# Batch 1's fifth group of attention weights turned by TensorE in place of a transposing DMA, and the eighth group's turn one step earlier

## The chip, the cores and the metric

The kernel runs on one core of one Trainium2 chip. The metric is the device time of one execution in microseconds, the median of several runs. The kernel before takes 306.03 us (three runs, 305.89 to 306.10).

A core has five engines with an instruction stream each: TensorE (PE: matmuls, with the weight load PEld beside it), VectorE (DVE), ScalarE (ACT), GpSimd (POOL) and SyncE (SP). Each works through its stream in order and waits on semaphores for the others. Here SP and POOL issue nearly all DMAs.

## The reference

Sliding-window causal attention, and behind it a two-layer network whose activation is h * cos(h):

```
scores = scale * np.matmul(q, k.transpose(0, 1, 3, 2))      # q, k, v: (8, 8, 576, 64)
rel = pos[:, None] - pos[None, :]
mask = (rel >= 0) & (rel < 64)
scores = np.where(mask, scores, -1e9)
attn = exp(scores - max) / (sum + 1e-09)
x = (attn @ v).transpose(0, 2, 1, 3).reshape(4608, 512)
h = x @ w_in                                                # (4608, 2048)
out = (h * np.cos(h)) @ w_out                               # (4608, 512)
```

## The kernel before, in words

**Two interleaved jobs.** The 4608 rows of x are cut into nine macro tiles of 512 rows. A macro tile `mt` runs the network: 16 column blocks of 128 of `h` (function `first`, four accumulating matmuls into a PSUM bank, L351), then `sin(h + pi/2)` on ACT (L527) and `h * sin` on DVE (L530), giving `gT`; then the second product, 64 matmuls `out_ps` (L542) into the two banks O0 and O1, copied out and stored. Attention for the batches ahead is put between these matmuls, so that PE always has something to do.

**Groups and units.** Eight batches, four head pairs `p` each, nine 64-row blocks `j` per batch. A unit is (batch, pair, block): two heads side by side, a 128x128 tile of scores. Groups hold three or four units. In the stage that this change touches (macro tile 0, getting ready macro tile 1) there are twelve groups, counted here from one, while the code's `i` counts from zero: the first (last block of batch 0) and the second (block 6 of batch 1) have four units, the third to the tenth have three (blocks 0 to 2 and 3 to 5 of one pair each), the eleventh and twelfth have four (blocks 7 and 8). In order of pairs: third = pair 0 blocks 0 to 2, fourth = pair 1 blocks 0 to 2, fifth = pair 0 blocks 3 to 5, sixth = pair 1 blocks 3 to 5, seventh and eighth = pairs 2 and 3 blocks 0 to 2, ninth and tenth = pairs 2 and 3 blocks 3 to 5.

**Steps of a group.** Scores on PE (`burst`, L261); on DVE, mask and maximum (`g_max`, L277); on ACT, exponential and sum (`g_exp`, L288); on DVE, the reciprocal of the sums (`g_inv`, L295); on POOL, the normalised bf16 weights `w` (`g_norm`, L302; on DVE for the first two groups). Then `w` has to be turned, since the product with the values needs it transposed (`wT`). `g_trans` has two ways: a group whose index is in `direct` is turned by PE, one 128x128 transpose per unit against the identity into a PSUM tile `tw_ps` (L311), and `g_put` copies that on DVE to SBUF as `wT` (L109); all others are turned by one DMA that SP issues (L314). `values(mt, p)` multiplies `wT` with the values for one pair (16 small matmuls, L330), and `put_x` copies the result to `xT` (on ACT for pair 1, on DVE for the others, L109), which is the operand of the `h` matmuls.

**Where the order comes from.** Nothing reorders instructions: `at(time, fn, ...)` puts a step on a list with a planned time, and `pump(time)` emits all steps up to a time between two column blocks or four `out_ps` matmuls. Steps emitted earlier stand earlier on every engine that they use. `LAGS` gives the distance of a group's steps from its scores, `DIRECT` names the groups that PE turns, `late` shifts the turn of some by one step, and `ready` says from when a unit's `wT` may be used, from which the time of `values` follows.

**Buffers.** PSUM has three rotating tiles with the tag `t` (`tw_ps`, `o_ps`), and the named banks X0, X1, S, O0, O1. The first five `h` blocks of macro tile 1 go into X0, X1, S, O0 and O1 in this order (`H_SECOND`), the last two of which hold macro tile 0's `out_ps` until DVE (O0) and ACT (O1) have copied them out.

**Loads.** POOL issues the DMAs that bring q, k (`rows`, L149) and v (L162) of later batches, in its one queue with the `w` of L302. SP issues the turns of `w`, the turns of a whole batch's q and k rows (`T`, L153), copies within v (L170) and the stores (L384).

Of the kernel before, what the change touches and what calls it, by code (L numbers as in the profile page):

```python
# [33 lines left out]
T = 2 * Q  # L34
LAGS = (0.2, 1, 3, 3.2, 3.8)
SKEW = 3
DIRECT = (0, 1, 5, 7, 8, 9)

# [11 lines left out]
def kernel(  # L52
# [18 lines left out]
    n_mt = B * S // MT  # L71
# [150 lines left out]
    groups = [[(0, p, j) for j in range(GF * g, GF * g + GF)] for p in range(PAIRS) for g in range(TU // GF)]  # L222
# [3 lines left out]
    for b, cuts in enumerate(CUTS, 1):  # L226
        for cut in cuts:
            for p0 in range(0, PAIRS, 2):
                for of, lo, hi in cut:
                    groups += [[(b, p, j) for p in range(p, p + of) for j in range(lo, hi)] for p in range(p0, p0 + 2, of)]  # L230
    direct = set(range(n_first)) | {n_first + i for i in DIRECT}

# [155 lines left out]
    def at(time, fn, *args):  # L388
        plan.append((time, len(plan), fn, args))
# [8 lines left out]
    ready = {(0, p, j): 0 for p in range(PAIRS) for j in range(TU)}  # L398
    n = n_first
    for t in range(B - 1):  # L400
        last = max(i for i, units in enumerate(groups) if units[0][0] == t + 1)
        time = T * t + Q - 1.4
        times = [time]
        for i in range(n, last + 1):
            times.append(times[-1] + PACE * len(groups[i]))
        if t:
            at(times[0], burst, n, BURSTS[0])
            at(times[4] + 0.1, burst, n + 4, BURSTS[1])
        else:
            for i in range(0, last + 1 - n, 2):  # L410
                at(times[max(i - 1, 0)] + (0.5 if i else 0), burst, n + i, (S_BANKS[i % 3], S_BANKS[(i + 1) % 3]))
        for i in range(last + 1 - n):
            time = times[i] + (0.3 if i > 3 and t else 0)
            lags = LAGS[:2] + tuple(T * t + T - 0.79 - time + 0.01 * s for s in range(3)) if n == last and t else LAGS
            if not t and i in (2, 3):
                lags = LAGS[:2] + (2.3, 2.5, LAGS[4])
            if not t and i == 9:
                lags = LAGS[:2] + (2.62, 2.63)
            for lag, fn in zip(lags, (g_max, g_exp, g_inv)):
                at(time + lag, fn, n)  # L420
            if t or i > 1:
                at(time + lags[3], g_norm, n)
            else:
                at(time + lags[2] + 0.01, g_norm, n, "d")
            late = 1 if not t and i in (5, 7) else 0
            at(time + (4.6 + late if n in direct else lags[-1]) if not t or i < 6 else T * t + T + 0.1 * i, g_trans, n)
            if n in direct:
                at(time + (4.62 if not t and i > 7 else 4.9) + late, g_put, n)
            ready.update({unit: time + (5.9 if n in direct else 8.5 if t else 9.6) for unit in groups[n]})
            n += 1  # L430

    for i, (name, p0) in enumerate((("q", 0), ("k", 0), ("q", 2), ("k", 2))):
# [16 lines left out]
    for mt in range(1, n_mt):  # L449
        for p in range(PAIRS):  # L450
            time = max(ready[b, p - p % 2 + i // TU, j] for i in range(2 * TU) for b, j in (divmod(mt * TU + i % TU, NU),))
            time = max(time, 25.5) if mt == 1 else T * mt - (8.01 if mt == n_mt - 1 else 1.01)
            at(time, values, mt, p)
            if mt == 1:
                at(time + 0.3 + 0.2 * (p % 2), put_x, mt, p, "a" if p == 1 else None)
            else:
                at(time + 0.2 + 0.1 * p, put_x, mt, p, "a" if p == 1 else None)
# [127 lines left out]
```

## Time and profile before

| what | value |
| --- | --- |
| median of three runs | 306.03 us (305.89 to 306.10) |
| the profiled execution | 306.36 us, of it 304.3 us span |
| PE busy | 292.8 us, 96% of the span |
| ACT busy | 235.6 us, 77% |
| DVE busy | 218.5 us, 72% |
| POOL busy | 170.9 us, 56% |
| granted TensorE clock | 0.999 |
| turns of `w` by DMA | 66, of them six in the stage of macro tile 1 |

The span is the time from the first to the last instruction of the profiled execution; some 2 us of the device time lie outside it. PE is busy for nearly all of the span, so the span can shrink by what PE waits, or by what it need not do. The page's chain of waits goes back from the last instruction to what released each step. A row of the timeline gives the start, the time taken, the engine, the line, the operation, the number of merged instructions, and in brackets the idle time before it with its releaser. Matmuls overlap in the pipeline, so the distance from one start to the next tells more of what an instruction costs than its own duration.

### The profile page before, as it was taken

What the parts mean: (1) busy time and instruction counts of PE and PEld (TensorE: products, weight loads), DVE (VectorE), ACT (ScalarE), POOL (GpSimd) and SP (SyncE); (2) the same over time, 40 slices, a digit from 0 to 9 for tenths busy, and PEclk for the clock granted to TensorE, in tenths of its full rate; (3) what the DMA queues carried; (4) which work ended last, traced back from release to release, by engine and by line L of the source; (5) the groups of instructions that cost most, each with busy time, mean ns of one, the idle gap of its engine ahead of it and who ended that gap; (6) DMA issues with size and microseconds to landing.
All of it is one profiled execution on the core that took longest, in us unless ns stands there. A gap on an engine that the chain in (4) does not pass through costs nothing.

```text
span 304.3 us, 7982 instructions
## 1 busy us (share of the span) xinstructions
PE 292.8 (96%) x2696; PEld 146.8 (48%) x2736; DVE 218.5 (72%) x834; ACT 235.6 (77%) x786; POOL 170.9 (56%) x198
## 2 busy tenths in 40 slices
PE   7899999899999999999999999999999999999996
PEld 6665444444454444444544444444444454454443
DVE  3877888678787878787877787778788877236701
ACT  5998799877997799679987998799869986106600
POOL 8996249794667867695649864977443630000000
PEclk9999999999999999999999999999999999999999
DMA  7999999999969996999999999999994433011011
GB/s 150 176 211 207 207 154 175 146 143 221 149 136 148 212 171 125 155 188 206 123 153 172 207 135 170 152 216 132 166 142 156 85 81 112 0 72 70 2 69 69
DMA packets 165577, 43.88 MB, mean 144 GB/s; under 512 B 154720, under 2 KB 160800, under 8 KB 165536
## 3 DMA queue, kind: packets, MB, share of 16 engines
q0 software_dynamic: 99344, 18.06, 76.1%
q1 hardware_dynamic: 66048, 25.11, 42.6%
q8 instruction: 21, 0.34, 0.5%
q10 hardware_dynamic: 144, 0.20, 0.2%
q14 instruction: 20, 0.16, 0.2%
HBM read 36.70 MB, written 9.44 MB: 152 GB/s over the span
## 4 chain that ended last, share of the span: by engine, by line
PE 73%; POOL 10%; DMA 9%; issue 4%; DVE 2%; ACT 1%; POOLq 0%; DVEq 0%
PE h_ps L351 37%; PE out_ps L542 30%; DMA w_out<-in_moe_w_out_dram 6%; POOL w L302 4%; DMA wT<-w 3%; PE o_ps L330 3%; PE s_ps L261 2%; POOL rows L142 2%; POOL rows L149 1%; POOL v L162 1%; PE out_ps L376 1%; POOL w_in L175 1%; POOL v L109 1%; DVE s L277 1%; ACT e L288 1%
## 5 line engine op out<-in xcount | busy, mean ns | idle before, releaser
L351 PE MATMUL h_ps<-xT,w_in 128*128 128x512 bf16 x557 | 125.9, 379 | 1.5 <-issue 0.3
L542 PE MATMUL out_ps<-w_out,gT 128*128 128x512 bf16 x542 | 123.0, 379 | 1.9 <-issue 1.1
L530 DVE TENSOR_TENSOR gT<-h_ps,sin 128x512 bf16<-128x512 f32 x144 | 95.4, 689 | 34.0 <-ACT sin L527 33.7
L527 ACT ACTIVATE sin<-h_ps 128x512 f32<-128x512 f32 x144 | 82.9, 599 | 34.2 <-PE h_ps L351 32.9
L288 ACT ACTIVATE e<-s,negm 128x128 f32<-128x128 f32 x256 | 98.6, 388 | 0.3 <-DVE negm L277 0.3
L302 POOL TENSOR_TENSOR w<-e,rden 128x512 bf16<-128x512 f32 (+1 forms) x76 | 74.7, 998 | 31.8 <-DVE rden L295 30.6
L351 PEld LDWEIGHTS <-w_in 128*128 128x128 bf16 x576 | 55.7, 98 | 65.7 <-issue 1.1
L542 PEld LDWEIGHTS <-gT 128*128 128x128 bf16 x560 | 53.2, 98 | 62.4 <-issue 0.2
L277 DVE CUSTOM_DVE_ANT_0 s<-s_ps,mask 128x128 f32<-128x128 f32 x256 | 58.0, 284 | 0.0
L288 ACT ACTIVATION_READ_ACCUMULATOR e<-s,negm 128x1 f32 x256 | 48.3, 189 | 0.0
L149 POOL DMA_DIRECT2D rows<-in_q_dram x30 | 25.5, 870 | 23.3 <-DMA T<-rows 13.9
L162 POOL DMA_DIRECT2D v<-in_v_dram x35 | 29.7, 877 | 10.5 <-DMA rows<-in_k_dram 7.5
L109 ACT COPY out_sb<-out_ps 128x512 f32<-128x512 f32 (+1 forms) x18 | 10.1, 564 | 24.7 <-PE out_ps L542 19.2
L295 DVE RECIPROCAL rden<-den 128x4 f32<-128x4 f32 (+1 forms) x80 | 13.8, 172 | 19.6 <-ACT e L288 18.2
L149 POOL DMA_DIRECT2D rows<-in_k_dram x30 | 25.5, 892 | 4.0 <-DMA rows<-in_q_dram 3.2
L109 DVE CAST xT<-o_ps 128x512 bf16<-128x512 f32 x27 | 17.5, 681 | 7.3 <-PE o_ps L330 7.0
L277 DVE DVE_READ_ACCUMULATOR2_ANT negm<- 128x1 f32 x256 | 21.2, 83 | 0.0
L109 DVE COPY out_sb<-out_ps 128x512 f32<-128x512 f32 x18 | 12.4, 689 | 12.0 <-PE out_ps L542 12.0
L288 ACT ACTIVATE e<-s_ps,negm 128x128 f32<-128x128 f32 x32 | 11.5, 425 | 1.9 <-DVE negm L273 1.4
L330 PE MATMUL o_ps<-wT,v 128*64 128x64 bf16 x504 | 11.4, 197 | 1.5 <-DMA wT<-w 1.4
L261 PEld LDWEIGHTS <-T 64*64 64x64 bf16 x512 | 8.2, 106 | 8.6 <-DVE negm L277 3.9
L330 PEld LDWEIGHTS <-v 128*64 128x64 bf16 x504 | 9.6, 112 | 5.8 <-issue 3.7
(58 smaller groups left out, 155.4 us busy)
## 6 DMA issues: line engine op xcount, KB each, us to landing
out_dram<-out_sb SPq DMA_DIRECT2D x16, 512.0 KB, 6.7
v<-in_v_dram POOLq DMA_DIRECT2D x28, 128.0 KB, 8.4
rows<-in_q_dram POOLq DMA_DIRECT2D x24, 128.0 KB, 5.9
rows<-in_k_dram POOLq DMA_DIRECT2D x24, 128.0 KB, 8.5
w_out<-in_moe_w_out_dram POOLq DMA_DIRECT2D x2, 1024.0 KB, 16.2
w_in<-in_moe_w_in_dram POOLq DMA_DIRECT2D x2, 768.0 KB, 12.5
wT<-w SPq DMA_TRANSPOSE x66, 4.5
out_dram<-out_sb SPq DMA_DIRECT2D x3, 256.0 KB, 2.0
```

Of the source, the lines that this page charges most:

```text
L109: {"a": nc.scalar.copy, "p": nc.gpsimd.tensor_copy}.get(engine, nc.vector.tensor_copy)(out, in_)
L149: nc.gpsimd.dma_start(out=rows(b)[lo:lo + n, slot * 512:slot * 512 + 512].rearrange("p (h d) -> p h d", h=H), in_={"q": q, "k": k}[name][b ...
L162: nc.gpsimd.dma_start(out=vt.rearrange("p (h d) -> p h d", h=H), in_=v[b, :, c * 128:c * 128 + n, :].rearrange("h p d -> p h d"))
L261: nc.tensor.matmul(out=s_ps[cross][to, u].rearrange("p (a t) -> p a t", a=2), lhsT=q_cols(b, p, j)[d], rhs=k_cols(b, p, j)[d], start=True, ...
L277: nc.vector.tensor_tensor_reduce(out=s[:, u], in0=s_ps[:, u], in1=mask[:, 2 - j % 2 if j else 0], scale=-scale if b else -1.0, scalar=BIG, ...
L288: nc.scalar.activation(e[:, u], s[:, u], AF.Exp, bias=negm[:, u:u + 1], scale=1.0 if n < n_first else -1.0, accum_out=den[:, u:u + 1])
L302: (nc.gpsimd if engine == "p" else nc.vector).tensor_tensor(out=w[:, 0:u], in0=e[:, 0:u], op=ALU.mult, in1=rden[:, 0:u].unsqueeze(2).to_br ...
L330: nc.tensor.matmul(out=o_ps[64 * h:64 * h + 64, 64 * i:64 * i + 64], lhsT=values_of(b)[:, max(j - 1, 0), 128 * p + 64 * h:128 * p + 64 * h ...
L351: nc.tensor.matmul(out=st["h", ff], lhsT=w_in_sb[:, ks, ff * 128:ff * 128 + 128], rhs=st["xT", mt][:, ks], start=start, stop=stop)
L527: nc.scalar.activation(sin, h_ps, AF.Sin, bias=math.pi / 2.0)
L530: nc.vector.tensor_tensor(out=gt[:, e], in0=h_ps, in1=sin, op=ALU.mult)
L542: nc.tensor.matmul(out=o_ps[e], lhsT=gT[ff // 2][:, ff % 2, ms * 128:ms * 128 + 128], rhs=w_out_sb[:, ff], start=ff == 0, stop=ff == n_ff - 1)
```

## The change

```
-DIRECT = (0, 1, 5, 7, 8, 9)
+DIRECT = (0, 1, 4, 5, 7, 8, 9)
...
-            late = 1 if not t and i in (5, 7) else 0
+            late = 1 if not t and i in (4, 5) else 0
             at(time + (4.6 + late if n in direct else lags[-1]) if not t or i < 6 else T * t + T + 0.1 * i, g_trans, n)
             if n in direct:
                 at(time + (4.62 if not t and i > 7 else 4.9) + late, g_put, n)
-            ready.update({unit: time + (5.9 if n in direct else 8.5 if t else 9.6) for unit in groups[n]})
+            ready.update({unit: time + (5.9 + late if n in direct else 8.5 if t else 9.6) for unit in groups[n]})
...
-            time = max(time, 25.5) if mt == 1 else T * mt - (8.01 if mt == n_mt - 1 else 1.01)
+            time = max(time, 29.5) if mt == 1 else T * mt - (8.01 if mt == n_mt - 1 else 1.01)
```

The fifth group (index 4) joins the groups that PE turns, and its turn comes one step late. The eighth (index 7) loses its late step. The planned time of pairs 0 and 1's `values` was set by the fifth group's DMA (19.78 + 9.6 = 29.38) and is now held at 29.5; its place among PE's instructions stays. Each turn by PE brings a copy on DVE with it.

On PE, in the second half of macro tile 0, around the scores of the last two groups (`s_ps`). The rows `w_...` with L311 are turns; the fifth group's `w` is w_1180. Rows of before; there the sixth group's `w` is w_1221, the eighth's w_1277 and the ninth's w_1302:

```order
L542 MATMUL out_ps_1189<-w_out_78,gT_702 128x512
L261 LDWEIGHTS T_790 [waits DVE_49]
L261 MATMUL s_ps_1253<-T_790 64x128 [waits PE_49]
...
L542 MATMUL out_ps_1189<-w_out_78,gT_729 128x512
L311 LDWEIGHTS w_1221 [waits Pool_49]
L311 MATMUL tw_ps_1284<-ident_79,w_1221 128x128
...
L542 MATMUL out_ps_1188<-w_out_78,gT_961 128x512
L311 LDWEIGHTS w_1277 [waits Pool_49]
...
L311 LDWEIGHTS w_1302 [waits Pool_49]
```

The same place in the changed kernel; the sixth group's `w` is now w_1219, the eighth's w_1281, the ninth's w_1306:

```order
L542 MATMUL out_ps_1189<-w_out_78,gT_702 128x512
L311 LDWEIGHTS w_1180 [waits Pool_49]
L311 MATMUL tw_ps_1244<-ident_79,w_1180 128x128
...
L261 LDWEIGHTS T_790 [waits DVE_49]
L261 MATMUL s_ps_1257<-T_790 64x128 [waits PE_49]
...
L311 LDWEIGHTS w_1219 [waits Pool_49]
...
L542 MATMUL out_ps_1188<-w_out_78,gT_846 128x512
L311 LDWEIGHTS w_1281 [waits Pool_49]
...
L311 LDWEIGHTS w_1306 [waits Pool_49]
```

Three turns of the fifth group stand ahead of the last scores, and the eighth group's turns stand four `out_ps` matmuls before the ninth's instead of directly ahead of them.

On PE a little later, inside pair 0's `values`, at the first use of the fifth group's `wT` (wT_1199 before). Rows of before:

```order
L330 LDWEIGHTS v1_75 [waits DMAHW3_49,DMAHW2_49]
L330 MATMUL o_ps_1350<-wT_1144,v1_75 64x64
L330 LDWEIGHTS v1_75 [waits DMASW3_49]
L330 MATMUL o_ps_1350<-wT_1199,v1_75 64x64 [waits DMAHW6_49]
L330 LDWEIGHTS v1_75
```

And of the change, where the fifth group's `wT` is wT_1253:

```order
L330 LDWEIGHTS v1_75 [waits DMAHW3_49,DMAHW2_49]
L330 MATMUL o_ps_1356<-wT_1144,v1_75 64x64
L330 LDWEIGHTS v1_75 [waits DMASW3_49]
L330 MATMUL o_ps_1356<-wT_1253,v1_75 64x64
L330 LDWEIGHTS v1_75
```

The wait on the DMA semaphore (DMAHW6) at this matmul is gone; nothing else in front of it has moved.

On DVE, between the tenth group's maxima and the eighth group's reciprocal (one piece of the difference):

```order
 L277 ISA s,negm<-s_ps,mask 128x128
 L277 ISA negm 128x1
+L109 COPY wT<-tw_ps 128x384
 L295 RECIPROCAL rden<-den 128x3
 L277 ISA s,negm<-s_ps,mask 128x128
```

The fifth group's copy out of PSUM is new there; the eighth group's copy moves from behind the twelfth group's maxima to a place ahead of them.

## The prediction

> **What bounds the kernel now.** I read the page's busy table and the chain of waits, then PE's waits by stretch, then the timeline of PE, POOL, SP, ACT and DVE between 49 and 61 us, where the change acts.
>
> ```profile
> PE 292.8 (96%) x2696; PEld 146.8 (48%) x2736; DVE 218.5 (72%) x834; ACT 235.6 (77%) x786; POOL 170.9 (56%) x198
> PE o_ps L330 <- DMA wT<-w: 0.7, 1, 0.7
> PE out_ps L542 <- issue: 1.1, 7, 0.2
> ```
>
> The second row is what the waits of PE give for 20 to 64 us, and the same row comes once more for 92 to 123 us; the third is PE's only other entry from 60 us to the end. So PE is the bound, and behind 20 us it loses noticeable time to another engine or to a DMA in two places alone, each of them a `values` matmul that waits for a turned `w`. The chain of waits runs over the first:
>
> ```profile
> 51.15 5.49 DMA wT<-w
> 56.64 0.04 issue
> 56.68 0.57 PE o_ps L330 x24
> ```
>
> PE's timeline around it (start, us, what):
>
> ```profile
> 49.42 1.90 PE L542 MATMUL out_ps<-w_out,gT 128*128 128x512 bf16 x8
> 51.25 0.42 PE L261 MATMUL s_ps<-T 64*64 64x128 bf16 x16
> 51.60 1.04 PE L542 MATMUL out_ps<-w_out,gT 128*128 128x512 bf16 x4
> 52.47 0.33 PE L311 MATMUL tw_ps<-ident,w 128*128 128x128 bf16 x3
> 52.64 1.89 PE L542 MATMUL out_ps<-w_out,gT 128*128 128x512 bf16 x7
> 54.36 0.51 PE L311 MATMUL tw_ps<-ident,w 128*128 128x128 bf16 x6
> 54.71 1.03 PE L542 MATMUL out_ps<-w_out,gT 128*128 128x512 bf16 x4
> 55.66 0.32 PE L330 MATMUL o_ps<-wT,v 128*64 128x64 bf16 x8
> 56.68 0.57 PE L330 MATMUL o_ps<-wT,v 128*64 128x64 bf16 x24 [0.70 <-DMA wT<-w]
> 57.18 0.34 PE L311 MATMUL tw_ps<-ident,w 128*128 128x128 bf16 x3
> 58.22 1.24 PE L351 MATMUL h_ps<-xT,w_in 128*128 128x512 bf16 x5
> 59.40 0.69 PE L330 MATMUL o_ps<-wT,v 128*64 128x64 bf16 x32
> 60.02 1.25 PE L351 MATMUL h_ps<-xT,w_in 128*128 128x512 bf16 x5
> ```
>
> Eight matmuls of pair 0 run (block 8 of batch 0, blocks 0 to 2 of batch 1: the first and third groups), and the ninth, on the fifth group, waits. 32 of these matmuls with no wait take 0.62 us (59.40 to 60.02), 0.0194 each. With no wait pairs 0 and 1 would have gone from 55.66 to 56.28; the next instruction starts at 57.18. The place costs 0.90 us, not the 0.70 in the brackets, because starts that overlap in the pipeline hide some 0.2.
>
> **What the change removes.** The fifth group's DMA and the wait on it. What is late next is the fourth group's DMA: pair 1 needs it from its third matmul on, the 19th of the 32. SP's rows for the fourth and the fifth, and the landing of the third and fourth (two DMAs: lowest, median, highest; the third's alone is 4.8):
>
> ```profile
> 49.86 1.25 SPq L314 DMA_TRANSPOSE wT<-w  x1
> 51.15 1.25 SPq L314 DMA_TRANSPOSE wT<-w  x1
> DMA to landing us min/median/max: 4.8/5.6/6.4
> ```
>
> The fourth lands at 49.86 + 6.4 = 56.26. SP issues it before the fifth's, which is the one taken out, so I keep 56.26; with the 0.04 of the chain PE can go on at 56.30.
>
> **What it adds on PE.** Three turns. Turns in a row cost 0.17 for three (52.47 to 52.64) and 0.35 for six (54.36 to 54.71). Parting the eighth group's from the ninth's adds none. So +0.17.
>
> *A rule against it.* The Trainium skill (TensorE: Matmul & The Clock Gate, Part 4: PE-mode transpose) measured about 275 ns for one such transpose inside a kernel. By it three would be an estimated 0.83 us, and little of the gain would be left. The rows above disagree: at 0.058 us from start to start they run pipelined, and the measurement decides; a rival below prices turns that do not overlap.
>
> **Do the turns wait for POOL?** POOL's `w` of the fifth, eighth and ninth groups:
>
> ```profile
> 50.13 0.84 POOL L302 TENSOR_TENSOR w<-e,rden 128x384 bf16<-128x384 f32 x1
> 52.49 0.82 POOL L302 TENSOR_TENSOR w<-e,rden 128x384 bf16<-128x384 f32 x1
> 53.65 0.83 POOL L302 TENSOR_TENSOR w<-e,rden 128x384 bf16<-128x384 f32 x1 [0.34 <-DVE rden L295]
> ```
>
> The fifth's is done at 50.97, and PE comes to it at 51.25: 0.28 to spare. Then, 0.17 later each: scores at 51.42, four `out_ps` from 51.77, the sixth group's turns at 52.64, four more, the eighth's at 52.81 + 0.87 = 53.68 (its `w` is done at 53.31, 0.37 to spare), four more, the ninth's at 53.85 + 0.87 = 54.72 (`w` at 54.48, 0.24 to spare). The eighth is the one that moves ahead, by 0.68 against 54.36. Where a slack is used up, each further tenth is a tenth of PE, with the last scores queued behind; I cost it at zero.
>
> **What it adds on DVE.** One copy of 0.35, ahead of the eighth group's reciprocal, for which POOL's `w` at 52.49 waits.
>
> ```profile
> 51.79 0.08 DVE L277 DVE_READ_ACCUMULATOR2_ANT negm<- 128x1 f32 x1
> 52.10 0.18 DVE L295 RECIPROCAL rden<-den 128x3 f32<-128x3 f32 x1 [0.23 <-ACT e L288]
> 53.06 0.35 DVE L109 COPY wT<-tw_ps 128x384 bf16<-128x384 bf16 x1
> 54.41 0.18 DVE L295 RECIPROCAL rden<-den 128x3 f32<-128x3 f32 x1 [0.90 <-ACT e L288]
> ```
>
> DVE is free from 51.87 and waits for ACT until 52.10. The turns run from 51.25 to 51.42 and are through the pipeline at about 51.64 (a turn takes 0.22), so the copy runs from 51.87 to 52.22 and the reciprocal comes 0.12 later, at 52.40 done: before the 52.49 at which POOL is free. The next maxima move by 0.12, the sixth's copy and the ninth's reciprocal with them, unless the overlap of DVE's instructions swallows it; the ninth's `w` would then end at 54.60, still ahead of 54.72. The 0.90 idle before 54.41 takes up the rest and the eighth's copy is taken in behind it. If that cover were gone, 0.1 to 0.35 would be PE's at the ninth's turns.
>
> **The sum on PE.** Pair 0 starts at 55.66 + 0.17 = 55.83; the 19th matmul would come at 55.83 + 18 x 0.0194 = 56.18, waits 0.12 for the fourth group, and the last 14 take 0.27: the tenth group's turns start at 56.57 instead of 57.18, 0.61 earlier.
>
> **What gives some of it back.** ACT does not move with PE here:
>
> ```profile
> 56.97 0.39 ACT L288 ACTIVATE e<-s,negm 128x128 f32<-128x128 f32 x1
> 57.35 0.57 ACT L109 CAST xT<-o_ps 128x512 bf16<-128x512 f32 x1
> 58.42 0.58 ACT L109 COPY out_sb<-out_ps 128x512 f32<-128x512 f32 x1 [0.51 <-PE out_ps L542]
> ```
>
> Its exponentials fill it up to 57.35 whatever PE does, pair 1's cast ends at 57.92, and only then can it copy O1, which the fifth `h` matmul needs. Before, the copy ended at 59.00 and that matmul started at 58.22 + 4 x 0.216 = 59.08 (0.216: twelve `out_ps` from 51.60 to 54.36, less 0.17 of turns). Now the copy goes from 57.92 to 58.50 and the matmul comes at 58.58, not at 59.08 - 0.61 = 58.47. So 0.50 is left, at most 0.55 if the copy starts a little before the cast's end, as the cast did after its exponential. The 0.51 of idle time on ACT was the cover; it is just used up. Pair 0's cast on DVE comes earlier with PE.
>
> Behind 60 us PE has work without a break until 121, so 0.50 passes through. Span 304.3 - 0.50 = 303.8; the profiled execution 306.36 would be 305.86; it stands 0.33 above the median, so against the median I forecast 306.03 - 0.50 = **305.53**. The bounds: 0.72 if the fourth lands early and ACT's copy does not bind (0.90 less 0.17), 0.35 if 0.15 is lost at the ninth's turns.
>
> **Rivals.**
>
> The second place where PE waits for a turned `w`, in macro tile 3:
>
> ```profile
> 108.57 0.69 POOL L162 DMA_DIRECT2D v<-in_v_dram  x1 [2.41 <-DMA rows<-in_k_dram]
> 109.27 3.04 POOL L302 TENSOR_TENSOR w<-e,rden 128x512 bf16<-128x512 f32 x3
> 121.05 0.47 PE L330 MATMUL o_ps<-wT,v 128*64 128x64 bf16 x18 [0.66 <-DMA wT<-w]
> ```
>
> POOL stands behind a load whose queue slot waits for a k load, so its `w` of that batch start late. (a) *Eaten later*: if those loads do not come 0.50 earlier, PE's wait grows from 0.66 to 1.16, and the time is 306.0. Against it: the loads go back to `T`, which SP turns behind the `w` of the batch before, all fed by PE's scores. (b) *That wait shrinks*: the loads from 59.74 us on are issued earlier, since POOL's last `w` of this stage follows DVE and PE; if the k load lands relatively sooner, up to 0.66 more is gained: 304.9. Nothing in the rows but the size of POOL's 2.41 wait speaks for it.
>
> (c) *Slower*: the fourth group's DMA becomes the long wait. The landing of the six DMA turns between 30 and 70 us:
>
> ```profile
> DMA to landing us min/median/max: 4.3/5.9/7.9
> ```
>
> At 7.9 the fourth would land at 57.76; PE goes on at 57.80, the last 14 end at 58.07, 0.89 after 57.18: 306.92. The point from which it decides is 7.0 us (49.86 + 7.0 + 0.04 + 0.27 = 57.17). For it: 6.4 is already the longest of those issued by 53 us. Against: everything ahead of it in the queues stays.
>
> (d) *The turns don't overlap*, 0.22 each: +0.66 in place of 0.17, pair 0 starts at 56.32, the tenth's turns at 56.94: 0.24 gained, 305.79.
>
> **How the numbers follow.** Forecast 48%, its own range 305.3 to 305.7; (a) 11%, (b) 18%, (c) 19%, (d) 4%. 0.2%, about what a measurement can tell from no change here, is 0.61 us: faster means below 305.42, slower above 306.64. A third of the forecast's chance lies below 305.42 (the bound of 0.72, and part of (b) with it): 16%, with (b) 34% faster. (c) 19% slower. The rest, 32 + 11 + 4 = 47%, same. The range that leaves out 2 in 10 takes in (b) and (a) and the first half of (c): 304.7 to 306.4.
>
> **What would show it.** Right: the `o_ps` row near 56 us has no wait or one of about 0.1, on the fourth group's DMA; the tenth's turns start at 56.5 to 56.7; ACT's copy of O1 follows the cast without idle time; the `h` matmuls after pairs 2 and 3 start at 59.5 instead of 60.02; the wait near 120.5 us is 0.66 again. Wrong: an idle time on POOL's `w` ahead of L311, a wait over 0.5 at the 19th `values` matmul, or more than 1 us at 120.5.

## The result, and the profile after

| | before | with the change | ratio, 95% interval |
| --- | --- | --- | --- |
| first comparison | 306.10 us (16 runs) | 304.91 us (16 runs) | 0.9970 [0.9957, 0.9983] |
| repeated later (`f1_after`) | 305.75 us (35 runs) | 304.99 us (12 runs) | 0.9972 [0.9959, 0.9985] |
| repeated once more (`g3_after`) | 305.78 us (23 runs) | 305.11 us (12 runs) | 0.9984 [0.9969, 0.9998] |

The change makes the kernel faster, by 0.3% in the first two comparisons and 0.16% in the third: 1.19, 0.76 and 0.67 us, where 0.50 was forecast. Single executions of the kernel before lie between 304.5 and 306.9 us but for three outliers, those with the change between 304.4 and 306.8, so one run of each would not have told; the ratios here and below leave out the highest of those outliers, 605.71 us, and one execution of `e3_after_v`, 380.29 us at a granted clock of 0.756.

The busy table of the change's page, PE's longest wait from 20 to 64 us (second row) and its only one from 92 to 123 us (third row):

```profile
PE 291.8 (96%) x2699; PEld 145.6 (48%) x2739; DVE 219.0 (72%) x835; ACT 235.5 (78%) x786; POOL 170.3 (56%) x198
PE tw_ps L311 <- POOL w L302: 0.3, 1, 0.3
PE out_ps L542 <- issue: 0.2, 1, 0.2
```

PE's wait for a turned `w` is in neither place any more; a wait of 0.3 us for POOL is new. PE's timeline of the change around the first place (start, us, what), to be held against the one in the prediction:

```profile
51.36 0.34 PE L311 MATMUL tw_ps<-ident,w 128*128 128x128 bf16 x3 [0.33 <-POOL w L302]
52.86 0.33 PE L311 MATMUL tw_ps<-ident,w 128*128 128x128 bf16 x3
53.03 1.03 PE L542 MATMUL out_ps<-w_out,gT 128*128 128x512 bf16 x3
53.89 0.33 PE L311 MATMUL tw_ps<-ident,w 128*128 128x128 bf16 x3
56.05 0.72 PE L330 MATMUL o_ps<-wT,v 128*64 128x64 bf16 x32
56.69 0.34 PE L311 MATMUL tw_ps<-ident,w 128*128 128x128 bf16 x3
57.73 1.24 PE L351 MATMUL h_ps<-xT,w_in 128*128 128x512 bf16 x5
59.53 1.69 PE L351 MATMUL h_ps<-xT,w_in 128*128 128x512 bf16 x7
```

Pairs 0 and 1 now run as one block of 32 from 56.05, and the `h` matmuls behind pairs 2 and 3 start at 59.53 instead of 60.02: 0.49 us. The second place, in macro tile 3, on PE:

```profile
118.78 1.41 PE L330 MATMUL o_ps<-wT,v 128*64 128x64 bf16 x64
120.22 4.04 PE L351 MATMUL h_ps<-xT,w_in 128*128 128x512 bf16 x17
```

Before, these 64 matmuls were cut at 121.05 by a wait of 0.66 and the `h` matmuls began at 121.45 (121.05 and the 0.40 of the last 18). From the `h` matmuls of macro tile 1 to the start of these 64 both kernels take the same (60.02 to 119.26 before, 59.53 to 118.78 now: 59.24 and 59.25), so the 1.23 us at 120.22 are 0.49 from the first place and 0.74 from the second. Behind it nothing changes: the span went from 304.3 to 303.1. POOL ahead of the second place:

```profile
106.31 0.69 POOL L162 DMA_DIRECT2D v<-in_v_dram  x1 [0.66 <-DMA rows<-in_k_dram]
107.38 1.03 POOL L302 TENSOR_TENSOR w<-e,rden 128x512 bf16<-128x512 f32 x1 [0.38 <-DVE rden L295]
```

The last v load waits 0.66 instead of 2.41 for what the prediction calls its queue slot, and POOL's first `w` starts at 107.38 instead of 109.27: 1.89 earlier, where PE is 0.49 earlier. In the trace that slot is a DMA semaphore. POOL's loads count on eight semaphores in turn, and this load has to wait until the second k load, which counts on the same one, has landed. That k load was issued at 98.17 and had landed at 108.04 before; with the change it was issued at 98.58 and had landed at 105.78.

SP carries the delay on to PE. Its six turns of `w` in that stage, before and with the change:

```profile
110.35 8.57 SPq L314 DMA_TRANSPOSE wT<-w  x6
```

```profile
108.44 9.42 SPq L314 DMA_TRANSPOSE wT<-w  x6
```

Before, the first one starts when POOL's first `w` is done (109.27 and 1.04), and all six follow close behind one another. POOL has caught up with DVE by 112.48, SP has not: its last turn starts at 117.72, although the `w` for it was done at 117.07, and lands at 121.01, just before PE goes on at 121.05. With the change the last turn starts at 116.65, when its `w` is done (116.58).

### The profile page after: what moved, and what is told of

Read it like the earlier page. It is cut to its first block, busy times and chain, and to the rows that moved or that the text cites. A ratio compares the mean times of both kernels' runs of the same rounds, so it can differ in the third digit from the quotient of the medians.

```text
span 303.1 us, 7987 instructions
## 1 busy us (share of the span) xinstructions
PE 291.8 (96%) x2699; PEld 145.6 (48%) x2739; DVE 219.0 (72%) x835; ACT 235.5 (78%) x786; POOL 170.3 (56%) x198
## 4 chain that ended last, share of the span: by engine, by line
PE 86%; DVE 4%; POOL 4%; issue 2%; DMA 2%; ACT 1%; POOLq 0%; DVEq 0%
PE h_ps L351 41%; PE out_ps L542 36%; PE o_ps L330 3%; PE s_ps L261 3%; DMA v<-in_v_dram 2%; DVE s L277 1%; PE out_ps L376 1%; POOL rows L142 1%; POOL v L162 1%; PE tw_ps L311 1%; POOL w L302 1%; POOL v L109 1%; ACT e L288 1%; DVE w L302 0%; DVE out_sb L109 0%
## 5 line engine op out<-in xcount | busy, mean ns | idle before, releaser
L109 ACT COPY out_sb<-out_ps 128x512 f32<-128x512 f32 (+1 forms) x18 | 10.1, 563 | 24.5 <-PE out_ps L542 19.0
L261 PE MATMUL s_ps<-T 64*64 64x128 bf16 x512 | 12.1, 221 | 0.0
```

The costliest lines, as they stand in the source:

```text
L109: {"a": nc.scalar.copy, "p": nc.gpsimd.tensor_copy}.get(engine, nc.vector.tensor_copy)(out, in_)
L261: nc.tensor.matmul(out=s_ps[cross][to, u].rearrange("p (a t) -> p a t", a=2), lhsT=q_cols(b, p, j)[d], rhs=k_cols(b, p, j)[d], start=True, ...
```

## The experiments

### Is the eighth group's move part of the gain? (`e1_late8`)

```
-            late = 1 if not t and i in (4, 5) else 0
+            late = 1 if not t and i in (4, 5, 7) else 0
```

> The change with the eighth group's turn left where it was before (directly ahead of the ninth's). My theory: that move is worth nothing, since six turns in a row cost 0.35 us and twice three cost 2 x 0.17, and the eighth group's weights are not awaited by anybody until pairs 2 and 3. Time as with the change, 304.9 us (within 0.3). Rival: parting the turns is part of the gain (a turn waits for POOL's weights when the six stand together, or the order of the copies on DVE matters): 0.3 to 0.6 us above the change, and a wait of PE's turns on POOL in the trace.

Measured: 304.79 us (12 runs), beside a kernel before of 305.35 (35 runs): 0.9983 [0.9965, 1.0002], an interval that takes in 1. Its timeline on PE:

```profile
54.45 0.50 PE L311 MATMUL tw_ps<-ident,w 128*128 128x128 bf16 x6
55.74 0.69 PE L330 MATMUL o_ps<-wT,v 128*64 128x64 bf16 x32
57.41 1.34 PE L351 MATMUL h_ps<-xT,w_in 128*128 128x512 bf16 x5
59.31 2.55 PE L351 MATMUL h_ps<-xT,w_in 128*128 128x512 bf16 x10
```

Six turns stand together, none waits, and 59.31 is no later than the change's 59.53. The eighth group's move brings nothing that these runs can see.

### Is the second wait POOL's queue? (`e2_before_v`, `e3_after_v`)

The kernel before, and the change, with batch 3's last v load put behind the `w` of its stage:

```
-            at(t0 + (0.5 if b == 2 else 14) + 0.8 * c, load_v, b, c)
+            at(t0 + (33 if (b, c) == (3, 4) else (0.5 if b == 2 else 14) + 0.8 * c), load_v, b, c)
```

> The kernel before, with one load moved: batch 3's fifth v load goes behind the weights of that stage in POOL's queue. My theory: the second wait (0.66 us at 121 us) comes from POOL standing behind this load, whose queue slot waits for a k load. The wait goes, the first (0.7 us near 56.7 us) stays: 306.1 - 0.66 = 305.4 us. Rival: the weights of that stage are late for another reason (the DMA that turns them, or the k load itself): the wait stays, 306.1 us.

> The change, with the same load moved. My theory: the second wait is already gone in most executions of the change, so the move adds little to the median: 304.6 to 304.9 us, with less spread; against the kernel before with the load moved, the first wait alone is left as the difference, 0.5 us. Rival: the change's gain is one effect and the load's move another, which add up: 304.9 - 0.66 = 304.2 us.

Measured: `e2_before_v` 305.51 us, 1.0009 [0.9979, 1.0038] against the same 35 runs of before; `e3_after_v` 304.88 us, 0.9989 [0.9973, 1.0005]. PE in the profile of `e2_before_v`:

```profile
55.15 0.32 PE L330 MATMUL o_ps<-wT,v 128*64 128x64 bf16 x8
56.76 0.57 PE L330 MATMUL o_ps<-wT,v 128*64 128x64 bf16 x24 [1.29 <-DMA wT<-w]
60.10 1.69 PE L351 MATMUL h_ps<-xT,w_in 128*128 128x512 bf16 x7
119.34 1.41 PE L330 MATMUL o_ps<-wT,v 128*64 128x64 bf16 x64
```

POOL's first `w` there follows DVE instead of a load:

```profile
107.94 1.03 POOL L302 TENSOR_TENSOR w<-e,rden 128x512 bf16<-128x512 f32 x1 [2.08 <-DVE rden L295]
```

SP's last turn of the stage starts at 117.18 instead of 117.72, although PE is no earlier than before (60.10). The second wait is gone and the first is still there, as my theory has it, and its 305.57 for the profiled execution fits. But the median is not under that of the kernel before beside it. That session's kernel before was already lower than in the first one (305.35 against 306.10), which was not profiled there, so this pair says where the wait comes from and leaves open what the move is worth. On the change the move gains nothing; the two effects don't add up as the rival had it (304.2). In the profile of `e3_after_v` the fourth group's DMA holds PE, as my rival (c) had it, though for less: the `h` matmuls start 0.18 us later than before (60.20 and 60.02), where (c) had 0.89.

```profile
51.41 0.34 PE L311 MATMUL tw_ps<-ident,w 128*128 128x128 bf16 x3 [0.22 <-POOL w L302]
57.02 0.41 PE L330 MATMUL o_ps<-wT,v 128*64 128x64 bf16 x14 [0.45 <-DMA wT<-w]
60.20 1.47 PE L351 MATMUL h_ps<-xT,w_in 128*128 128x512 bf16 x6
```

### Does the second wait come back when PE is late? (`e4_pad`, `f4_pad_v`)

Nine matmuls of the identity behind the tenth group's turns, with unused results:

```
-    nc.vector.memset(small, 0.0)
+    nc.vector.memset(small, 0.0); at(29.94, warm, "X1", 9)
```

> The change, with nine matmuls of the identity (results unused) behind the tenth group's turns, some 0.5 us of PE, so that PE reaches the h matmuls of macro tile 1 when it did before. Theory A: the second wait went because everything behind 57 us comes 0.5 us earlier against the loads; now it comes back, 306.0 us. Theory B: it went because the fifth group's DMA is no longer in SP's queue, which moves the later DMAs whatever PE does; it stays away, 304.9 + 0.5 = 305.4 us.

Measured: 305.96 us (12 runs, none under 305.64), 1.0024 [1.0009, 1.0039]. PE and POOL in its profile:

```profile
60.07 1.69 PE L351 MATMUL h_ps<-xT,w_in 128*128 128x512 bf16 x7
121.12 0.47 PE L330 MATMUL o_ps<-wT,v 128*64 128x64 bf16 x18 [0.69 <-DMA wT<-w]
```

```profile
95.52 4.25 POOL L149 DMA_DIRECT2D rows<-in_q_dram  x5 [4.54 <-DMA T<-rows]
108.30 1.66 POOL L162 DMA_DIRECT2D v<-in_v_dram  x2 [1.70 <-DMA rows<-in_k_dram]
109.97 5.14 POOL L302 TENSOR_TENSOR w<-e,rden 128x512 bf16<-128x512 f32 x5
```

With PE back at 60.07 the second wait is back, 0.69, and the time is theory A's. The route is not that of before: POOL's loads begin 2.2 us later than before (95.52 against 93.30), and two v loads stand ahead of the `w`. They are also 1.3 us later against PE than with the change (95.52 - 60.07 against 93.70 - 59.53), because SP's turns of batch 3's rows, whose landing POOL waits for, take longer than in either kernel (4.67 before, 6.09 with the change):

```profile
87.81 6.69 SPq L153 DMA_TRANSPOSE T<-rows  x2
```

So the premise of theory B, that the later DMAs run otherwise without the fifth group's DMA, holds here too, and this run does not show that 0.5 us of PE alone brings the wait back. The same kernel with both of these loads behind the `w`:

```
-            at(t0 + (0.5 if b == 2 else 14) + 0.8 * c, load_v, b, c)
+            at(t0 + (30 + c if b == 3 and c > 2 else (0.5 if b == 2 else 14) + 0.8 * c), load_v, b, c)
```

> The change with the nine matmuls of padding, which brought the second wait back (0.69 us in the profile, 305.96 us), and batch 3's fourth and fifth v loads behind the weights of that stage in POOL's queue. My theory: the wait comes from POOL standing behind these loads, so it goes although PE is as late as before: 305.4 us, the change plus the padding. Rival: the weights are late for another reason: the wait stays, 306.0 us.

In this kernel the copies within v (on DVE for this batch) read batch 3's fourth piece before it is loaded, so a part of that batch's values is not the reference's; the instructions are the same in number. Measured: 305.08 us, 0.9980 [0.9967, 0.9994] beside a kernel before of 305.75, where `e4_pad` stood at 1.0024. PE and POOL:

```profile
59.32 2.55 PE L351 MATMUL h_ps<-xT,w_in 128*128 128x512 bf16 x11
118.56 1.64 PE L330 MATMUL o_ps<-wT,v 128*64 128x64 bf16 x64
```

```profile
107.16 1.03 POOL L302 TENSOR_TENSOR w<-e,rden 128x512 bf16<-128x512 f32 x1 [0.53 <-DVE rden L295]
```

The wait is gone, POOL's `w` follow DVE again. PE is earlier in this execution, too (59.32, in spite of the padding), so the single profile does not part the two causes. The medians do better, since the slowest of its 12 runs (305.65) is under the kernel before beside it (305.75) and the fastest of `e4_pad` (305.64) above its own (305.35). They differ by 0.88 us, more than the wait of 0.69, so they do not measure the wait alone. Together with `e2_before_v`, where PE is as late as before, they show that the second wait arises in POOL's queue.

### How much is the first place worth? (`f1_after`, `g1_before`, `g2_before`, `g3_after`)

Both kernels unchanged, run and profiled again.

> The change itself once more, beside the kernel before on this chip, since the kernel before came out at 305.35 us where three of its variants ran (35 runs, 304.5 to over 306), against 306.10 earlier. My theory: the kernel before sits at one of two levels, with and without the second wait (0.7 us), and the change stays at the lower one: the change 304.9 us, 0.4 to 1.2 us under the kernel before by how often that shows the wait. Rival: the 1.2 us measured first is the size of the effect and the kernel before is again at 306.1.

> The kernel before, one more profile. My theory: the fifth group's DMA pins PE near 56.7 us however early PE arrives, so the h matmuls behind pairs 2 and 3 start at 60.0 to 60.1 us again, with a wait of 0.7 to 1.3 us for that DMA. Rival: that start varies from execution to execution as it does with the change (58.96 to 60.20 us over seven profiles).

> The same once more; the second wait (near 121 us) may be there or not, and where it is not, the time is about 305.4 us instead of 306.1.

> The change, beside the kernel with the third k load moved, on the same chip: 304.9 us.

The times of `f1_after` and `g3_after` are in the first table; the single executions of the kernel before took 306.11 and 306.42 us. PE in the two profiles of the kernel before, first `g1_before`:

```profile
56.60 0.57 PE L330 MATMUL o_ps<-wT,v 128*64 128x64 bf16 x24 [0.73 <-DMA wT<-w]
59.94 1.90 PE L351 MATMUL h_ps<-xT,w_in 128*128 128x512 bf16 x8
120.88 0.47 PE L330 MATMUL o_ps<-wT,v 128*64 128x64 bf16 x18 [0.57 <-DMA wT<-w]
```

and `g2_before`:

```profile
56.70 0.57 PE L330 MATMUL o_ps<-wT,v 128*64 128x64 bf16 x24 [0.74 <-DMA wT<-w]
60.04 1.68 PE L351 MATMUL h_ps<-xT,w_in 128*128 128x512 bf16 x7
121.13 0.47 PE L330 MATMUL o_ps<-wT,v 128*64 128x64 bf16 x18 [0.73 <-DMA wT<-w]
```

With the first profile and `e2_before_v` that makes four in which the fifth group is turned by DMA: the `h` matmuls start at 60.02, 60.10, 59.94 and 60.04, although PE reached pair 0 anywhere from 55.15 to 55.66. The DMA pins them; this rests on `e2_before_v` in the main, since the other three reached pair 0 between 55.55 and 55.66. PE in `f1_after`:

```profile
55.49 0.69 PE L330 MATMUL o_ps<-wT,v 128*64 128x64 bf16 x32
58.96 2.33 PE L351 MATMUL h_ps<-xT,w_in 128*128 128x512 bf16 x10
```

and in `g3_after`:

```profile
57.44 1.34 PE L351 MATMUL h_ps<-xT,w_in 128*128 128x512 bf16 x5
59.33 2.33 PE L351 MATMUL h_ps<-xT,w_in 128*128 128x512 bf16 x10
```

With the turn on PE the start follows PE: 59.53, 59.31 (`e1_late8`), 58.96, 59.33, and 60.20 where the fourth group's DMA was late (`e3_after_v`). Against the 60.02 of the first profile that is a gain of 0.49, 0.71, 1.06 and 0.69 us, and a loss of 0.18. The second wait stood in all three profiles of the kernel before (0.66, 0.57, 0.73) and in none of the change (first profile, `f1_after`, `g3_after`). These three executions took 306.11 to 306.42 us, like the 306.10 of the first comparison; what the kernel before does in its executions of 304.5 to 305.3 us no profile caught. How much of the difference between the medians (1.19, 0.76 and 0.67) is the second place stays open.

The 0.69 of `g3_after` did not last. From the `h` matmuls of macro tile 1 to the `values` of macro tile 3 PE took 59.79 us there (59.33 to 119.12), 0.55 more than the 59.24 or 59.25 of the other profiles. The 64 `values` matmuls of macro tile 2 took 2.06 us from 87.69 on (1.44 in `f1_after`). Two of them start at 88.44 and 89.24, 0.04 behind the landings of the last two of SP's six turns there. So the kernel with the change can still wait for a turned `w`, at a third place.

### A version that may beat both (`f2_kload`, `f3_kload_v`, `g4_kload`)

In three profiles with the fifth group on PE its turns wait for POOL (0.33, 0.22 in `e3_after_v`, 0.46 in `e4_pad`). POOL issues a k load of 0.94 us directly ahead of that `w`; here it goes behind it. `f3_kload_v` has the v load of `e3_after_v` moved as well.

```
-            at(t0 - T + ((19.4, 19.41, 22, 28.6)[c] if b == 2 else 10.5 + 0.9 * c) if c < 4 else
+            at(t0 - T + ((19.4, 19.41, 23, 28.6)[c] if b == 2 else 10.5 + 0.9 * c) if c < 4 else
```

> The change, with the third k load of batch 2 issued by POOL behind the fifth group's weights instead of ahead of them. My theory: in three of four profiles of kernels with the change PE's turns of the fifth group wait 0.2 to 0.5 us for these weights, because POOL spends 0.94 us on that load first. The wait goes; since pairs 0 and 1 then come to the fourth group's DMA earlier, 0 to 0.3 us are gained: 304.6 to 304.9 us. Rival: POOL's load comes too late for batch 2's rows and stalls later work: 305.5 us or more.

> As the last, and batch 3's fifth v load behind the weights of its stage as well, which takes away what can be taken of both waits. My theory: 304.5 to 304.8 us, with the smallest spread. Rival: the v load, issued later, holds up the loads behind it: over 305 us.

> The change, with the third k load of batch 2 behind the fifth group's weights, again. My theory: it takes away the wait of PE's turns for POOL, which the change shows in some executions: 0.1 to 0.4 us under the change beside it. Rival: the 0.36 us between the two earlier were noise: the same time.

Measured: `f2_kload` 304.63 us, 0.9968 [0.9953, 0.9983]; `g4_kload`, the same kernel again, 304.78 us, 0.9966 [0.9942, 0.9990]; `f3_kload_v` 305.03 us, 0.9980 [0.9964, 0.9995]. Beside the change on the same chip the k load's move stands 0.36 (304.99) and 0.33 us (305.11) lower, twice the same way, but the intervals of the ratios overlap widely, so it is not told apart from the change. Its POOL does what was meant, three `w` in a row and then the load:

```profile
47.43 2.61 POOL L302 TENSOR_TENSOR w<-e,rden 128x384 bf16<-128x384 f32 x3
49.99 0.94 POOL L149 DMA_DIRECT2D rows<-in_k_dram  x1
```

A part of the wait moves to the eighth group's turns, whose `w` comes later now: in `f2_kload` they start 1.01 us behind the four `out_ps` matmuls ahead of them (52.39 to 53.40), in the change 0.86 (53.03 to 53.89). Moving the v load on top gains nothing. I had expected the smallest spread of it, but it is larger (304.63 to 306.48) than that of `f2_kload` (304.43 to 305.57).

## Why the prediction was right and where it was not

**What bounds the kernel** was right: PE, with two waits for a turned `w`; the 1.23 us between the two profiles are those two.

**The turns' cost** was right: with the sixth group's turns 52.86 to 53.03, 0.17 us for three. The fifth group's own turns add the same: from the four `out_ps` matmuls ahead of the last scores to the four behind them it is 1.31 us before (50.29 to 51.60) and 1.48 in `e1_late8` (50.21 to 51.69). Rival (d) falls. By the 275 ns each that the Trainium skill gives (TensorE: Matmul & The Clock Gate, Part 4: PE-mode transpose) three would have been an estimated 0.83 us; the trace does not agree.

**"I cost it at zero", the turns' wait for POOL**, held in `e1_late8`, `f1_after` and `g3_after`, and did not in the first profile of the change. There POOL reached the fifth group's `w` at 50.46 instead of 50.13, since all its row of loads had run later, and PE came earlier; the 0.28 to spare became a wait of 0.33. The slack was that of one execution, in which PE's and POOL's starts happened to lie so.

**The copy on DVE** was hidden as forecast. In the change's profile:

```profile
51.74 0.36 DVE L109 COPY wT<-tw_ps 128x384 bf16<-128x384 bf16 x1 [0.16 <-PE tw_ps L311]
52.02 0.17 DVE L295 RECIPROCAL rden<-den 128x3 f32<-128x3 f32 x1
```

The eighth group's reciprocal starts at 52.02, even a little ahead of the 52.10 of before.

**The fourth group's DMA as the next wait**: I put 0.12 for it. It was 0.45 in one of five profiles of the change and its two close relatives (`e1_late8`, `e3_after_v`), and none in the other four.

**ACT gives some back**: the mechanism is there. In `e1_late8` ACT's copy follows the cast with no idle time,

```profile
57.28 0.56 ACT L109 CAST xT<-o_ps 128x512 bf16<-128x512 f32 x1
57.74 0.58 ACT L109 COPY out_sb<-out_ps 128x512 f32<-128x512 f32 x1
```

and the five `h` matmuls there and in `g3_after` take 1.34 us instead of 1.24. In the change's first profile it did not bind, since PE was held at 51.36 and the copy waited 0.31 for PE. So the sum of 0.50 met the 0.49 of that profile by luck, by errors that cancel (POOL's wait in, the fourth's wait and ACT's delay out). Over the four profiles without a wait for the fourth group's DMA the first place is worth 0.49 to 1.06, 0.74 on average, and the term was sized too small. (The upper bound, 0.90 less 0.17, is 0.73 and not 0.72.)

**The forecast itself**, 305.53 with its own range of 305.3 to 305.7, was missed in the first comparison: 304.91 lies below that range, and inside 304.7 to 306.4 only because rival (b) had a chance. The gains of the two repeats, 0.76 and 0.67, are nearer to the 0.50.

**The step that failed** is "the wait near 120.5 us is 0.66 again", with "0.50 passes through". It did pass through, and the second wait went as well: rival (b), which had 18% and 304.9 us. I had written that nothing but the size of POOL's wait of 2.41 spoke for it. What the runs show in its place: POOL's loads of that stage land sooner with the change (the k load that the last v load waits for took 7.20 us instead of 9.87), so POOL and behind it SP start on that stage's `w` sooner. `e2_before_v` shows that the second wait hangs on that place in POOL's queue, and `e4_pad` that it can come back with the change, when the loads begin later. Why the loads land sooner is not settled (below). Rival (a) has the opposite sign of what happened; (c) showed once, in `e3_after_v`, with a wait of 0.45 where its landing at 57.76 would have meant 1.62 (56.18 to 57.80).

## What to carry to other kernels

A wait for a DMA's landing can pin everything behind it to the DMA, and the bracket in one profile shows what it cost in that execution alone: without it the stage follows its own engine, here 0.5 to 1.1 us earlier in four profiles, and no earlier in a fifth, where the next DMA was late. Slack between two engines whose starts drift apart from run to run (0.28 us here) has to be held against that drift before it is costed at zero. And where the profile shows the same kind of wait a second time further on, it deserves its own sum. Here the delay went from the semaphore of one load through POOL's queue, which holds loads and computation, and SP's turns to PE, and it changed by more (1.89 us at POOL) than the edit moved PE (0.49).

## What the runs showed of the hardware that was not expected

With one DMA fewer in SP's queue near 51 us, DMAs some 40 us later run otherwise, and in the same way in every profile. The view of DMA issues between 93 and 103 us gives for the q and k loads (KB each, median us to landing) before:

```profile
rows<-in_q_dram POOLq DMA_DIRECT2D x4, 128.0 KB, 6.8
rows<-in_k_dram POOLq DMA_DIRECT2D x4, 128.0 KB, 9.8
```

and with the change:

```profile
rows<-in_q_dram POOLq DMA_DIRECT2D x4, 128.0 KB, 5.1
rows<-in_k_dram POOLq DMA_DIRECT2D x4, 128.0 KB, 8.5
```

In the four profiles with the fifth group's DMA the q loads take 6.4 to 7.3 us, and the k loads 9.4 to 10.1; in the eight without it that have no padding 4.5 to 5.1 and 7.7 to 8.5. Among the eight is `e3_after_v`, where PE is as late as before (60.20), so it is not PE's earlier start that does it. The two turns of batch 3's rows, which SP issues just before, behave the other way: before and with the change

```profile
87.76 4.67 SPq L153 DMA_TRANSPOSE T<-rows  x2
```

```profile
87.27 6.09 SPq L153 DMA_TRANSPOSE T<-rows  x2
```

they take 4.66 to 4.68 us in the four and 5.92 to 6.27 in the eight. The two turns of batch 2's rows at 54 us, close behind the DMA that is taken out, differ too: 10.1 to 11.2 us in the four, 7.6 to 8.7 in all ten without it. So the loads start some 0.9 us later against PE (93.70 - 59.53 against 93.30 - 60.02) and are through sooner. Which of the two, the later start or less company in the DMA engines, makes them faster was not tried. In the two padded kernels they start later still (95.52 and 95.19), the q loads take 5.8 and 5.9 us and the k loads 8.3 and 8.5, so a later start does not always make them faster.
